# Sigmoid attention and a mixture-of-depths block on one core: values loaded earlier into borrowed tiles, an earlier ranking, shared sums, and the last spot transfer on SyncE

## The chip, the cores and the metric

The kernel runs on one core of a Trainium2 chip. The metric is the device time of the program in microseconds, as the median of several runs; smaller is better. The kernel before takes 488.92 us (three runs, 486.96 to 489.0). Its profiled execution took 486.84 us, of which 485.0 us lie between the first and the last instruction. All times on the profile's clock count from that first instruction.

## The reference

Two stages follow each other, all in float32. The first is attention with a sigmoid in place of the softmax, over 8 batches (called blocks here), 12 heads, 448 tokens and 64 numbers per head:

```python
scores = scale * np.matmul(q, k.transpose(0, 1, 3, 2)) - np.log(S)
attn = 1.0 / (1.0 + np.exp(-scores))
attn_out = np.matmul(attn, v)
x = attn_out.transpose(0, 2, 1, 3).reshape(B, S, H * D)   # 8 x 448 x 768
```

The second picks, in each block, the 128 tokens with the largest score `x @ w_gate`, sends only those through a two-layer network (768 to 1024 to 768, with a ReLU between), weights the result with the sigmoid of the score and adds it to those rows. All other rows of `x` go to the output as they are:

```python
scores = np.einsum('bsd,d->bs', x, w_gate)
top_idx = np.argpartition(-scores[b], capacity)[:capacity]
xe = x[b, top_idx]
ye = np.maximum(xe @ w1, 0.0) @ w2
out[b, top_idx] = xe + sigmoid(scores[b, top_idx])[:, None] * ye
```

## The kernel before

**Steps and units.** The 12 heads of a block are three groups of four heads. Two groups make a step `s`, so there are 12 steps (0 to 11), and a block ends after one and a half steps. A step has seven units `n` (0 to 6). `unit(s, n)` multiplies keys with queries for a part of the key rows of both groups (line 280) and lets ScalarE put the sigmoid into tiles `attn_d` and `attn_u` (line 288). `values(s, n)` multiplies these with v in four quarters (line 315): quarter 0 runs in the last unit of its own step, quarters 1 to 3 in the units 0 to 2 of the next step. After quarter 3 VectorE takes the result out of the two banks `o` by transposes (`take`, line 330), and `gate_part` sums it against `w_gate` (lines 338 and 341).

**Loads.** Keys and queries of group `i` come through `load(i)` (line 100) and are turned on VectorE by `turn(i)` into `kT` and `qT` (lines 255 to 262). Values of step `s` come through `load_v(s)`: four transfers into `raw_v` (line 119) and four into `raw_h` (line 121). Both tiles exist once, so v of a step can be loaded only when quarter 3 of the step before has read the old one. For that reason `load_v(s)` stands in unit 3 of step `s`, and v is wanted in unit 6 of the same step. All of these are issued by SyncE in the order of the program. Each issue also waits until the transfer which had its completion counter before, eight transfers earlier in most cases, has landed.

**Routing.** When the last group of block `b` is done, `gate(b)` forms the 448 scores and GpSimd writes them to DRAM (line 366); `spread` reads them back as `rep`, once for every partition (line 378). `ranking` compares (`rank`, lines 386 and 389), and `place` turns the ranks, writes them to DRAM as `ranks` (line 399) and reads them back for every partition as `spot` (line 401). `choose` finds from `spot` which row goes to which of the 128 places (line 413), and GpSimd gathers these rows of `x_d`, a copy of `x` in DRAM, into a tile `xe` (line 426). There are three `xe` tiles; the last block uses an attention tile instead. In `routed` the steps of this chain are put into fixed units of later steps.

**The network.** Two blocks form a pair `p`. `turn_rows` transposes the gathered rows on TensorE (line 448). Both layers are multiplied with seven products of half-size blocks in place of eight: `first` (line 487) and `second` (line 552), with sums on VectorE. Six of the quarters of `w1` and `w2` lie in SBUF (`w1_sb`, `w2_sb`). The other eight operands are sums of quarters. `make_sum` forms each once on VectorE (line 172) in a region of the tile `hidden` or `rows_t`, and GpSimd writes it to DRAM (line 174). The table `SUMS` says in which unit. Later `lend` loads a sum into attention tiles that are free in that step (line 188), and `weight` hands it to a product and forgets it. The tables `WORK` and `LENT` say which products and loads lie in which unit. Pairs 0 and 1 and the start of pair 2 run beside the attention.

**The end.** `rest` is written out by hand: the rest of pair 2, the routing of block 7, the products of pair 3, and the copies of blocks 6 and 7 to the output (line 351), followed by the scatter of the computed rows (line 572). An engine does its instructions in the order in which the program gives them.

Of the kernel before, what the change touches and what calls it, by code (L numbers as in the profile page):

```python
# [9 lines left out]
F32 = mybir.dt.float32  # L10
# [7 lines left out]
def kernel(  # L18
# [85 lines left out]
    def load_v(s):  # L104


        if s >= NS:
            return
        raw_v[s] = (vals.tile([P, 8, NF * Dh], F32, name="raw_v"),
                    vals.tile([P, 4, Dh], F32, name="raw_h"))  # L110
        tv, th = raw_v[s]

        def blocks(h, r, nh, n):
            return bass.AP(tensor=v.tensor,
                           offset=v.offset + (8 * s + h) * S * Dh + r * Dh,
                           ap=[[TB * Dh, TT], [S * Dh, nh], [1, n * Dh]])

        for m in range(4):
            nc.sync.dma_start(out=tv[m * TT:(m + 1) * TT], in_=blocks(0, NF * m, 8, NF))
        for n in range(4):  # L120
            nc.sync.dma_start(out=th[n * TT:(n + 1) * TT],
                              in_=blocks(4 * (n // 2), HK + n % 2, 4, 1))
# [3 lines left out]


    QW = KH * FH * P
    assert QW == FH * DH and QW % (2 * P) == 0 and FH * DH // 2 % DH == 0
    w1_sb = const.tile([P, 3, QW], F32, name="w1_sb")  # L130
    w2_sb = const.tile([P, 3, QW], F32, name="w2_sb")
# [20 lines left out]

    room = {}

    def load_left(m):

        if m == 1:
            t = moe.tile([P, 7 * FH * P], F32, name="hidden")
            room["a"], room["b"] = t[:, :QW], t[:, QW:2 * QW]
        load_quarter(m, room["a"], (1, 0) if m == 1 else (0, 1))  # L160

    def make_sum(m, key):
        if (m, key) == (1, 6):
# [11 lines left out]


    SUMS = {(1, 3): (1, 5), (1, 4): (1, 6), (1, 5): (1, 7), (1, 6): (1, 3),
            (2, 4): (2, 5), (2, 5): (2, 6), (2, 6): (2, 7), (3, 0): (2, 4)}

    def attn_tile(pr, slot):  # L180
        return attnp.tile([P, 2, S], F32, name=f"attn{pr}_{slot}")
# [7 lines left out]
            halves.append(t)  # L189
        lent[m, key] = halves  # L190

    def weight(m, key):

        if (m, key) in lent:
            halves = lent.pop((m, key))
            return lambda o, n: halves[2 * o // QW][:, o % (QW // 2):o % (QW // 2) + n]
        x = {(1, 1): 0, (1, 2): 1, (1, 4): 2, (2, 1): 0, (2, 2): 1, (2, 3): 2}[m, key]
        return lambda o, n: (w1_sb, w2_sb)[m - 1][:, x, o:o + n]
# [92 lines left out]
    def values(s, n):  # L291

        tv, th = raw_v[s]
        if n == 0:
            outs[s] = [banks(0), banks(1)]
        o = outs[s]
        first = (0, 2, 2, 0)[n]  # L300
        quads = [(first + m) % 4 for m in range(4)]
        work = [(r, c) for c in range(NF) for r in quads]
        if n < 2:
            at = 4 * (NF - 1)
            work[at:at] = [(r, None) for r in quads]
        for r, c in work:
            x, pr = divmod(r ^ n, 2)
            rows = slice(r * TT, (r + 1) * TT)
            for j in range(2):
                if c is None:  # L310
                    w, a = th[rows, 2 * pr + j, :], attn[s, pr, NF]
                else:
                    w = tv[rows, 4 * x + 2 * pr + j, c * Dh:(c + 1) * Dh]
                    a = attn[s, pr, (NF + 1) * x + c]
                nc.tensor.matmul(o[x][j * Dh:(j + 1) * Dh, pr, :S], w, a[rows, j, :],  # L315
                                 start=(n == 0 and c == 0), stop=(n == 3 and c == NF - 1))
        if n < 3:
            nc.scalar.activation(o[x][Dh:Dh + 1, pr, S:S + 1], bias_s[Dh:Dh + 1], AF.Copy)
        else:
            for x in range(2):  # L320
                for pr in range(2):
                    take(s, pr, x)
# [67 lines left out]
            out=junk[:n], in0=rep[:n], scalar=own, in1=earlier[:n, c, :],  # L390
            op0=ALU.is_equal, op1=ALU.mult, accum_out=level[:n, c:c + 1])

    def place(b):

        nc.vector.tensor_add(place_s[:, :NC], above, level)
        by_col = moe.tile([P, TT], F32, name="by_col")
        nc.vector.transpose(by_col, place_s)
        ranks = dram.tile([P, TT], F32, name="ranks")
        nc.gpsimd.dma_start(out=ranks, in_=by_col)
        spot = moe.tile([P, 4, NC * TT], F32, name="spot")  # L400
        nc.gpsimd.dma_start(
            out=spot, in_=bass.AP(tensor=ranks.tensor, offset=ranks.offset,
                                  ap=[[0, P], [TT * TT, 4], [1, NC * TT]]))
        st[b]["spot"] = spot.rearrange("p m c -> p (m c)")[:, :S]
# [72 lines left out]
    def first(p, key, where="o"):  # L477
        n = CAP
        x = pairs[p]["x"][:, ROWS1[key]]
        if key == 1:  # L480
            t = moe.tile([P, 7 * FH * P], F32, name="hidden")
            pairs[p]["h"] = t.rearrange("p (m k n) -> p m k n", m=7, k=FH)
        w = weight(1, key)
        ps = bank(where).rearrange("p (k n) -> p k n", n=P)
        for f in range(FH):
            for t in range(KH):
                nc.tensor.matmul(ps[:, f, :n], w((t * FH + f) * P, P), x[:, t, :n],  # L487
                                 start=(t == 0), stop=(t == KH - 1))
        if key == 2:
            pairs[p]["second"] = True  # L490
            last_row(p)
        return p, key, ps
# [53 lines left out]
    def second(p, key, where="o"):  # L546
        n = CAP
        h = pairs[p]["h"][:, ROWS2[key]]
        w = weight(2, key)
        ps = bank(where)  # L550
        for t in range(FH):
            nc.tensor.matmul(ps[:n, :DH], h[:, t, :n], w(t * DH, DH),  # L552
                             start=(t == 0), stop=(t == FH - 1))
        return p, key, ps
# [59 lines left out]
    def put(s, n, fn, *args):  # L614
        late.setdefault((s, n), []).append((fn, args))

    def routed(b):

        s = (NG * b + NG - 1) // 2 + 1
        if s == NS:  # L620
            return
        put(s, 4, spread, b)
        put(s, 4, store, b)
        put(s + 1, 1, ranking, b)
        if s + 2 <= NS:
            put(*((s + 2, 1) if b % 2 else (s + 1, 5)), copy_out, b)
            put(s + 2, 0, choose, b)

    def ranking(b):
        for c in range(NC):  # L630
            rank(b, c)
        place(b)

    def gates(i):
        gate_part(i)
# [26 lines left out]
    def rest():  # L662


        for n in range(3):
            gap(NS, n)
        p, b = NP - 2, B - 1
        for key, slot in (((1, 3), "d10"), ((2, 4), "d11")):
            lend(*key, slot)
        work = [(item, begin(item, "any")) for item in ((1, p, 6), (1, p, 7))]  # L670
        gates(2 * NS - 1)

        store(b, (0, 1))
        gate(waiting.pop())
        spread(b, nc.sync)
        store(b, (2, 3))
        for key, slot in (((2, 5), "d12"), ((2, 6), "u3"), ((2, 7), "u4")):
            lend(*key, slot)
        for item, args in work:
            finish(item, args)  # L680
        for key in (4, 5):
            do((1, p, key), "any")
        first_sums(*begin((1, p, 3), "any"), sums_too=())
        work = [((2, p, key), begin((2, p, key), "any")) for key in (2, 1, 4)]
        ranking(b)
        hidden_sum(p, 5)
        work.append(((2, p, 5), begin((2, p, 5), "any")))
        choose(b - 1)
        hidden_sum(p, 6)
        finish(*work[0])  # L690
        work.append(((2, p, 6), begin((2, p, 6), "any")))
        hidden_sum(p, 7)
        finish(*work[1])
        work.append(((2, p, 7), begin((2, p, 7), "any")))
        hidden_sum(p, 3)
        for item, args in work[2:]:
            finish(item, args)
        choose(b)
        do(("t", b - 1), "any")
        do((2, p, 3), "any")  # L700

        for key, slot in (((1, 3), "d12"), ((1, 6), "u3"), ((1, 7), "u4"), ((1, 5), "d00"),
                          ((2, 6), "d01"), ((2, 5), "d02"), ((2, 7), "d10"), ((2, 4), "d11")):
            lend(*key, slot)
        copy_out(b - 1)
        copy_out(b)
        p += 1
        for item in ((1, p, 1), (1, p, 2), ("t", b)):
            do(item, "any")
        work = [((1, p, key), begin((1, p, key), "any")) for key in (3, 6, 7)]  # L710
        for item, args in work[1:]:
            finish(item, args)
        first_sums(*work[0][1], sums_too=())
        for key in (4, 5):
            do((1, p, key), "any")
        for m in (5, 6, 7, 3):
            hidden_sum(p, m)
        for key in (1, 2, 6, 5, 3, 7, 4):
            do((2, p, key), "any")

    def stream():
# [14 lines left out]
        for s in range(NS):  # L736
            for n in range(NU):
                unit(s, n)
                if n == (0 if s == 0 else 1):
                    turn(2 * s + 1)  # L740
                    load(2 * s + 3)
                if n == 3 and s > 0:
                    load_v(s)
                gap(s, n)
                if n == NU - 2:
# [41 lines left out]
```

## Time and profile before

| | us | share of the span |
|---|---|---|
| median of the runs | 488.92 | |
| span of the profiled execution | 485.0 | |
| TensorE, matmul | 450.1 | 93% |
| TensorE, weight load (beside the matmuls) | 273.1 | 56% |
| VectorE | 298.9 | 62% |
| ScalarE | 181.6 | 37% |
| GpSimd | 50.1 | 10% |
| keys by queries, L280, 2496 matmuls | 154.5 | |
| attention by v, L315, 1152 + 1152 + 384 matmuls | 132.3 + 132.9 + 29.4 | |

Busy time is read as follows. Engines run beside each other, so the columns do not add to the span. Several of the small matmuls of L280 and L315 run in different parts of the array at once, and overlapping ones are counted once. The transfers of SyncE took 64.9% of the time of the 16 DMA engines over the span, those of GpSimd 12.5%. Together they moved 104.19 MB, most of it in small packets: 97344 of the 131085 packets are below 512 bytes.

Two kinds of view are used for the rest. A list of waits says which engine stood idle until which other had done something. A timeline gives instructions in the order of their start, with the idle time ahead of an instruction and what ended it in square brackets. "SPq" is the queue of SyncE: the time shown there is the issue of a transfer, with its waits for completion counters, and not the transfer itself. Where a wait is for several events, the one named is the one that came last by the profile.

### The profile page before, as it was taken

The numbers are of one execution on the slowest core, as the hardware profiler recorded it, in microseconds if no ns is written. First come the engines' busy times: TensorE is split into PE (matmuls) and PEld (weight loads), VectorE is DVE, ScalarE is ACT, GpSimd is POOL, SyncE is SP. The second block draws the span as 40 slices with busy tenths as digits, with TensorE's granted clock in tenths as the row PEclk, the third lists the DMA queues.
The fourth block names the chain that finished last, engine by engine and source line by source line (L and its number), as shares of the span: only waits on it lengthen the run. The fifth ranks groups of instructions, "written<-read, shape, count | busy, mean of one in ns | idle before, by whom it ended". The sixth has DMA issues, their size and how long they took to land. (4 is left out here: it accounts for less than half of the span.)

```text
span 485.0 us, 14374 instructions
## 1 busy us (share of the span) xinstructions
PE 450.1 (93%) x6326; PEld 273.1 (56%) x6326; DVE 298.9 (62%) x663; ACT 181.6 (37%) x237; POOL 50.1 (10%) x81
## 2 busy tenths in 40 slices
PE   8998979879999999999999999999999999748993
PEld 3553525426554664555477844685566386338951
DVE  4319495976552875985637576786618579812371
ACT  4746462443554345334355253344346201001100
POOL 8000001011000001011100000010100010210001
PEclk9999998999999999999999999999999999958999
DMA  8956998899948974999697848899459887998201
GB/s 262 325 219 168 372 284 252 229 203 238 250 128 301 211 179 102 269 184 336 154 333 199 141 158 225 160 256 318 130 175 244 134 197 155 277 354 305 97 0 65
DMA packets 131085, 104.19 MB, mean 215 GB/s; under 512 B 97344, under 2 KB 112000, under 8 KB 130768
## 3 DMA queue, kind: packets, MB, share of 16 engines
q1 hardware_dynamic: 126864, 86.75, 64.9%
q0 software_dynamic: 4160, 16.53, 12.5%
q8 instruction: 49, 0.80, 0.7%
q14 instruction: 12, 0.10, 0.1%
HBM read 82.67 MB, written 31.60 MB: 236 GB/s over the span
## 5 line engine op out<-in xcount | busy, mean ns | idle before, releaser
L280 PE MATMUL psc<-qT,kT 32*64 32x448 f32 x2496 | 154.5, 541 | 5.4 <-ACT attn_u L288 4.9
L315 PE MATMUL o<-attn_d,raw_v 32*64 32x448 f32 x1152 | 132.3, 543 | 2.9 <-DMA raw_v<-in_v_dram 2.3
L315 PE MATMUL o<-attn_u,raw_v 32*64 32x448 f32 x1152 | 132.9, 545 | 1.9 <-DMA raw_v<-in_v_dram 1.2
L288 ACT ACTIVATE attn_u<-psc,bias_s 128x896 f32<-128x896 f32 x86 | 81.9, 1004 | 83.1 <-PE psc L280 83.1
L280 PEld LDWEIGHTS psc<-qT,kT 32*64 32x64 f32 x2496 | 64.9, 131 | 64.7 <-issue 36.2
L288 ACT ACTIVATE attn_d<-psc,bias_s 128x896 f32<-128x896 f32 x70 | 66.7, 1003 | 49.2 <-PE psc L280 48.0
L330 DVE STREAM_TRANSPOSE x_b<-o 128x448 f32<-128x448 f32 x48 | 26.9, 617 | 79.5 <-PE o L315 79.5
L315 PEld LDWEIGHTS o<-attn_u,raw_v 32*64 32x64 f32 x1152 | 54.7, 133 | 30.0 <-issue 17.8
L315 PEld LDWEIGHTS o<-attn_d,raw_v 32*64 32x64 f32 x1152 | 50.5, 133 | 25.4 <-issue 15.3
L341 DVE TENSOR_REDUCE gate_p<-scr 128x14 f32<-128x448 f32 x48 | 29.8, 622 | 1.7
L552 PE MATMUL o<-attn_d,hidden 128*128 128x384 f32 x88 | 30.4, 492 | 0.0
L487 PEld LDWEIGHTS o<-rows_t,w_sb 128*128 128x128 f32 x240 | 27.6, 192 | 4.5 <-issue 1.4
L487 PEld LDWEIGHTS o<-rows_t,attn_d 128*128 128x128 f32 x240 | 27.5, 192 | 4.8 <-DVE rows_t L460 2.0
L338 DVE TENSOR_TENSOR scr<-x_b,wg_b 128x448 f32<-128x448 f32 x48 | 29.5, 614 | 1.0
L487 PE MATMUL o<-rows_t,attn_d 128*128 128x128 f32 x240 | 28.8, 277 | 1.2 <-DVE rows_t L460 1.2
L487 PE MATMUL o<-rows_t,w_sb 128*128 128x128 f32 x240 | 29.0, 278 | 0.4 <-DVE rows_t L454 0.3
L563 DVE SCALAR_TENSOR_TENSOR xe<-o,gate,xe 128x384 f32<-128x384 f32 x37 | 21.1, 612 | 13.4 <-PE o L552 13.3
L315 PE MATMUL o<-attn_u,raw_h 32*64 32x448 f32 x384 | 29.4, 555 | 0.0
L500 DVE TENSOR_TENSOR hidden<-o,hidden 128x512 f32<-128x512 f32 x23 | 15.3, 688 | 22.6 <-PE o L487 22.3
L255 DVE STREAM_TRANSPOSE kT<-raw_k 128x384 f32<-128x384 f32 x46 | 23.6, 552 | 7.4 <-DMA raw_k<-in_k_dram 3.8
L503 ACT ACTIVATE hidden<-hidden 128x512 f32<-128x512 f32 x12 | 7.5, 630 | 53.7 <-DVE hidden L500 53.7
L386 DVE TENSOR_SCALAR_CACHE_REDUCE scr<-rep,score 128x448 f32<-128x448 f32 (+1 forms) x32 | 21.5, 671 | 9.2 <-DMA rep<-scores 8.3
(102 smaller groups left out, 419.8 us busy)
## 6 DMA issues: line engine op xcount, KB each, us to landing
attn_d<-sum SPq DMA_DIRECT2D x56, 384.0 KB
x_d<-x_b SPq DMA_DIRECT2D x32, 336.0 KB
out_dram<-x_d SPq DMA_DIRECT2D x8, 1344.0 KB
raw_k<-in_k_dram SPq DMA_DIRECT2D x23, 448.0 KB
raw_q<-in_q_dram SPq DMA_DIRECT2D x23, 448.0 KB
raw_v<-in_v_dram SPq DMA_DIRECT2D x48, 192.0 KB
w_sb<-in_moe_w_dram SPq DMA_DIRECT2D x6, 768.0 KB
sum<-hidden POOLq DMA_DIRECT2D x6, 768.0 KB, 7.1
```

Of the source, the lines that this page charges most:

```text
L255: nc.vector.transpose(kT[i][:, e, :HK], sk[:, e, :HK].rearrange("p (m c) d -> p c m d", c=NF))
L280: nc.tensor.matmul(psc[h // 2][y * Dh:(y + 1) * Dh, h % 2, :S], kT[2 * s + x][d, e, r:r + 2, :].rearrange("d r t -> d (r t)"), qT[2 * s + ...
L288: nc.scalar.activation(a, psc[pr][:, :, :S], AF.Sigmoid, bias=bias_s, scale=QK_SCALE)
L315: nc.tensor.matmul(o[x][j * Dh:(j + 1) * Dh, pr, :S], w, a[rows, j, :], start=(n == 0 and c == 0), stop=(n == 3 and c == NF - 1))
L330: nc.vector.transpose(x_tiles[b][:, :, 2 * g + pr, :], outs[s][x][:, pr, :S].rearrange("p (r t) -> p r t", t=TT))
L338: nc.vector.tensor_tensor(out=tmp, in0=x_tiles[b][:, :, hp, :], in1=wg_b[:, hp:hp + 1, :].to_broadcast([P, TB, TT]), op=ALU.mult)
L341: nc.vector.tensor_reduce(out=gate_parts[b][:, :, hp], in_=tmp, axis=AX.X, op=ALU.add)
L386: nc.vector.tensor_scalar(out=junk[:n], in0=rep[:n], scalar1=own, scalar2=0.0, op0=ALU.is_gt, op1=ALU.add, accum_out=above[:n, c:c + 1])
L487: nc.tensor.matmul(ps[:, f, :n], w((t * FH + f) * P, P), x[:, t, :n], start=(t == 0), stop=(t == KH - 1))
L500: nc.vector.tensor_tensor(out=dst, in0=a, in1=b, op=ALU.add)
L552: nc.tensor.matmul(ps[:n, :DH], h[:, t, :n], w(t * DH, DH), start=(t == 0), stop=(t == FH - 1))
L563: nc.vector.scalar_tensor_tensor(out=xe[:n, cols], in0=ps[:n, :DH], scalar=st[b]["gate"][:n, 0:1], in1=xe[:n, cols], op0=ALU.mult, op1=ALU ...
```

## The change

There are four parts.

1. Values of steps 1 and 3 no longer go into `raw_v` and `raw_h` but into two of the three `xe` tiles (half of the heads each) and a free part of the first `hidden` tile, behind the two regions that the sums use. Those places are not needed by the routed blocks until later. So v alternates between two places in the first five steps, and `load_v` of steps 1 to 4 is issued one step earlier: that of step 1 at the end of step 0, those of steps 2, 3 and 4 in unit 3 of the step before. From step 5 on all is as it was. The main part of v comes in eight transfers in place of four in steps 1 and 3, with the same bytes.
2. The ranking of block 0 moves from unit 1 of step 3 to the last unit of step 2. Two of the sums, (2, 7) and (2, 4), move from unit 6 of step 2 and unit 0 of step 3 to units 4 and 5 of step 3.
3. The sums loaded for pair 2 stay in their tiles, and pair 3 uses them there. The eight `lend` calls for pair 3 in `rest`, which make 16 transfers of 384 KB, are gone.
4. In the routing of the last block SyncE issues the `spot` transfer, and no longer GpSimd.

Line numbers in the profile of the changed kernel are up to 18 higher than those above.

```diff
@@ load_v
-        raw_v[s] = (vals.tile([P, 8, NF * Dh], F32, name="raw_v"),
-                    vals.tile([P, 4, Dh], F32, name="raw_h"))
-        tv, th = raw_v[s]
+        if s in (1, 3):
+            tv = [moe.tile([P, D], F32, name="xe", bufs=3).rearrange("p (h c) -> p h c", h=4)
+                  for _ in range(2)]
+            at = 2 * QW + s // 2 * 4 * Dh
+            th = room["all"][:, at:at + 4 * Dh].rearrange("p (h c) -> p h c", h=4)
+        else:
+            t = vals.tile([P, 8, NF * Dh], F32, name="raw_v")
+            tv = [t[:, :4], t[:, 4:]]
+            th = vals.tile([P, 4, Dh], F32, name="raw_h")
+        raw_v[s] = (tv, th)
...
-            nc.sync.dma_start(out=tv[m * TT:(m + 1) * TT], in_=blocks(0, NF * m, 8, NF))
+            rows = slice(m * TT, (m + 1) * TT)
+            if s in (1, 3):
+                for x in range(2):
+                    nc.sync.dma_start(out=tv[x][rows], in_=blocks(4 * x, NF * m, 4, NF))
+            else:
+                nc.sync.dma_start(out=t[rows], in_=blocks(0, NF * m, 8, NF))
@@ SUMS
-            (2, 4): (2, 5), (2, 5): (2, 6), (2, 6): (2, 7), (3, 0): (2, 4)}
+            (2, 4): (2, 5), (2, 5): (2, 6), (3, 4): (2, 7), (3, 5): (2, 4)}
@@ weight
-    def weight(m, key):
+    def weight(m, key, p):
         if (m, key) in lent:
-            halves = lent.pop((m, key))
+            halves = lent[m, key]
+            if p != NP - 2:
+                del lent[m, key]
@@ place
-    def place(b):
+    def place(b, queue=nc.gpsimd):
...
-        nc.gpsimd.dma_start(
+        queue.dma_start(
             out=spot, in_=bass.AP(tensor=ranks.tensor, offset=ranks.offset,
@@ routed
-        put(s + 1, 1, ranking, b)
+        put(*((s, NU - 1) if b == 0 else (s + 1, 1)), ranking, b)
@@ rest
-        ranking(b)
+        ranking(b, nc.sync)
...
-        for key, slot in (((1, 3), "d12"), ((1, 6), "u3"), ((1, 7), "u4"), ((1, 5), "d00"),
-                          ((2, 6), "d01"), ((2, 5), "d02"), ((2, 7), "d10"), ((2, 4), "d11")):
-            lend(*key, slot)
         copy_out(b - 1)
         copy_out(b)
@@ stream
-                if n == 3 and s > 0:
+                if (n == NU - 1 and s == 0) or (n == 3 and s in (1, 2, 3)):
+                    load_v(s + 1)
+                elif n == 3 and s > 4:
                     load_v(s)
```

More of the change, by code (lines that the diff above doesn't have):

```diff
@@ L128 @@
     QW = KH * FH * P
+    assert D == 4 * NF * Dh and 2 * QW + 8 * Dh <= 7 * FH * P
     assert QW == FH * DH and QW % (2 * P) == 0 and FH * DH // 2 % DH == 0
@@ L153 @@
     room = {}
+    room = {}
     def load_left(m):
@@ L158, in load_left @@
             t = moe.tile([P, 7 * FH * P], F32, name="hidden")
-            room["a"], room["b"] = t[:, :QW], t[:, QW:2 * QW]
+            room["all"], room["a"], room["b"] = t, t[:, :QW], t[:, QW:2 * QW]
         load_quarter(m, room["a"], (1, 0) if m == 1 else (0, 1))
@@ L312, in values @@
                 else:
-                    w = tv[rows, 4 * x + 2 * pr + j, c * Dh:(c + 1) * Dh]
+                    w = tv[x][rows, 2 * pr + j, c * Dh:(c + 1) * Dh]
                     a = attn[s, pr, (NF + 1) * x + c]
@@ L482, in first @@
             pairs[p]["h"] = t.rearrange("p (m k n) -> p m k n", m=7, k=FH)
-        w = weight(1, key)
+        w = weight(1, key, p)
         ps = bank(where).rearrange("p (k n) -> p k n", n=P)
@@ L548, in second @@
         h = pairs[p]["h"][:, ROWS2[key]]
-        w = weight(2, key)
+        w = weight(2, key, p)
         ps = bank(where)
@@ L627, in routed, with ranking @@
             put(s + 2, 0, choose, b)
-    def ranking(b):
+    def ranking(b, *queue):
         for c in range(NC):
             rank(b, c)
-        place(b)
+        place(b, *queue)
     def gates(i):
```

## The prediction

> **What bounds the kernel now.** I began with the page. TensorE is busy for 93% of the span, so only its idle and slowed time can be won.
>
> ```profile
> PE 450.1 (93%) x6326; PEld 273.1 (56%) x6326; DVE 298.9 (62%) x663; ACT 181.6 (37%) x237; POOL 50.1 (10%) x81
> PEclk9999998999999999999999999999999999958999
> ```
>
> The next view is the list of waits of TensorE alone. The columns are total us, times, longest.
>
> ```profile
> PE o L448 <- DMA xe<-x_d,row: 8.3, 1, 8.3
> ...
> PE o L315 <- DMA raw_v<-in_v_dram: 3.5, 5, 1.3
> PE o L280 <- DVE x_b L330: 2.1, 1, 2.1
> ```
>
> One wait of 8.3 us stands out; the others are small, but a list of waits does not show slowed matmuls. So I took busy time in stretches: one each for steps 1, 2 and 3 of the attention (counted from 0), then two in the last part. After the stretch and its length come busy us of TensorE, weight load, VectorE, ScalarE and GpSimd, then TensorE's granted clock, DMA share and GB/s.
>
> ```profile
> 21.40:47.20 25.80, 24.38 (x466) 12.55 (x450) 11.87 (x18) 13.72 (x17) 1.20 (x2) 1.00 0.63 205
> 47.20:77.60 30.40, 26.98 (x460) 12.11 (x454) 22.64 (x38) 13.72 (x17) 3.23 (x6) 0.94 0.97 296
> 77.60:111.10 33.50, 28.02 (x460) 14.09 (x451) 25.03 (x62) 13.72 (x17) 4.51 (x7) 0.95 0.95 238
> ...
> 422.50:431.00 8.50, 0.25 (x2) 0.29 (x3) 2.65 (x8) 0.00 (x0) 1.00 (x1) 0.63 1.00 267
> 431.00:441.40 10.40, 10.40 (x62) 8.62 (x61) 0.62 (x1) 1.50 (x3) 1.97 (x2) 0.81 1.00 394
> ```
>
> Steps 1 to 3 hold the same TensorE work (460 to 466 matmuls), yet last 25.8, 30.4 and 33.5 us. Steps 2 and 3 lose 4.6 and 7.7 us against step 1: part is idle, part a TensorE clock of 0.94 and 0.95. DMA is 0.95 to 0.97 full there and 0.63 in step 1. The timeline says what ended the idle time:
>
> ```profile
> 60.55 4.02 SPq L119 DMA_DIRECT2D raw_v<-in_v_dram  x4
> 64.61 6.12 SPq L121 DMA_DIRECT2D raw_h<-in_v_dram  x4
> ...
> 71.49 1.62 PE L315 MATMUL o<-attn_d,raw_v 32*64 32x448 f32 x8 [1.27 <-DMA raw_v<-in_v_dram]
> ...
> 94.12 2.34 PE L280 MATMUL o<-qT,kT 32*64 32x448 f32 x26 [2.08 <-DVE x_b L330]
> ...
> 103.47 1.73 PE L315 MATMUL o<-attn_d,raw_v 32*64 32x448 f32 x8 [1.07 <-DMA raw_v<-in_v_dram]
> ```
>
> Step 2's v was issued from 60.55 to 70.7 for matmuls ready at 70.2. In step 1 that quarter of values takes 3.4 us (43.75 to 47.15). In step 2 it takes 7.4 (70.2 to 77.6), in step 3 8.7 (102.4 to 111.1): late v costs 4.0 and 5.3 us, slow matmuls included.
>
> Last, the timeline of the final part:
>
> ```profile
> 412.38 0.57 POOL L399 DMA_DIRECT2D ranks<-by_col  x1 [11.78 <-DVE by_col L397]
> ...
> 420.35 0.75 POOL L401 DMA_DIRECT2D spot<-ranks  x1 [7.41 <-DVE xe L563]
> 421.41 1.02 POOL L426 DMA_INDIRECT xe<-x_d,row  x1 [0.30 <-DMA attn_d<-sum]
> ...
> 428.82 0.69 DVE L413 SCALAR_TENSOR_TENSOR scr<-spot,slot,number 128x448 f32<-128x448 f32 x1 [5.15 <-DMA spot<-ranks]
> ...
> 430.75 1.51 PE L448 MATMUL o<-iden,xe 128*128 128x128 f32 x6 [8.26 <-DMA xe<-x_d,row]
> ```
>
> The gather of block 6's rows (L426) had its row numbers at 414.0, but stood on GpSimd behind the `spot` transfer of block 7, which waited for `ranks` to land. So it was issued at 421.4, landed 9.3 us later, and TensorE stood still from 422.5 to 430.75.
>
> **What the Trainium skill says.** "TensorE: Matmul & The Clock Gate", section "What's actually happening": about 3.4 us of idle time halve the clock until the array has been busy as long again. The trace agrees: after the 8.26 us gap eight matmuls of L552 take 4.20 us, elsewhere 2.74. "DMA: Bandwidth & Descriptors", section "Issuing engines are not separate DMA queues": transfers of all issuers share the same 16 DMA engines, so another issuer saves issue time alone. The trace can only half agree: here it is not issue time but the order behind a wait that costs. "Perfetto Trace Analysis", section "Tensor Engine Instruction (MATMUL, LD_WEIGHTS)": GpSimd and VectorE work strictly in order. The 7.4 us of L426 behind L401 are that.
>
> **The change part by part.** Times are on the clock of before.
>
> *`spot` of the last block on SyncE.* The gather can be issued right behind `ranks`, at about 414.1. The indirect gathers landed in 3.0 to 9.2 us, median 5.8; six loads of sums are still draining, so I take 8: 422.1, before TensorE wants it at 422.5 (ends: 417 and 423.3). SyncE has nothing else to do then but the two copies to the output, which wait for a scatter at 427 or later, so the new wait delays nobody. `ranks` lands at 420.3 as before, or some us sooner. No 256 KB `spot` on SyncE is in the trace; bounds are the 3.3 us from SyncE's `rep` of 224 KB (402.56) to its reader (405.88), and GpSimd's 6.8 to 8.6 us. I take 4: 424.3. Two selections and two conversions 1.5 us, gather at 425.8, landed after 5.8: 431.6. TensorE's road there: turning block 6 from 422.5, 0.9; one second-layer product 2.74; two first-layer products of 2.84 each: 431.8. It was 441.44: gain 9.6 us, that is 8.26 of wait and 1.4 of slow clock. At the slow bound `spot` costs 4 of them.
>
> *Shared sums.* 16 loads of 384 KB vanish from 414 on. TensorE shows no wait for them after 441, so alone they give nothing; they clear the road for `ranks`, `spot` and both gathers. Counted as 0.
>
> *v earlier.* Issued one step earlier for steps 1 to 4, v lies ready. v(1) goes behind the weights from 19 us and is needed at 43.75: free. v(2) goes out at about 35, where DMA is 0.63 full. v(3) takes the place of v(2) in the busy stretch, with eight main transfers for four, but nobody waits for it until about 100. Step 2: values end at 73.6 for 77.6. The next scores need qT of group 6, which VectorE finishes only at 74.5, as before: gain 3.1, not 4.0.
>
> *First ranking earlier.* On VectorE it now stands ahead of turn 7. Its `rep` was issued at 75.19 and needs 4.9 to 5.7 us: 80.5. VectorE then does 6.4 us of ranks (86.9), turn 7 in 2.2 (89.1), and the four transposes in 2.2 (91.3). TensorE wants turn 7 at 74.5 + 12.65 = 87.1: it waits 2.0, then 0.7 for its bank, against the 2.1 it waited for `x_b` before. So 0.6 is lost. The two sums (1.75 us each), moved behind it, sit where VectorE's next product, turn 8, is ready at 103.0, when TensorE arrives.
>
> *Step 3.* With v there, the 5.3 us go too. Step 4 starts at 103.0 for 111.1: 8.1 gained, or 3.1 - 0.6 + 5.3 = 7.8; I keep 8.
>
> *Step 4 gives some back.* Block 1's scores leave at 98.4 for 102.1, only 3.7 sooner (the transposes ahead of them start at 89.1 for 92.83); its `rep` landed 12.3 us later (114.4): 110.7. Ranks end at 116.9, the transposes that free the bank for turning block 0 at 119.1, where TensorE arrives at 117.2. I take 1.5; ends 0 and 5, the latter if the two moved sums (1.5 MB at 238 GB/s, 6 us) push `rep` back. From there on TensorE has no wait worth naming until 411, so what is gained stays.
>
> Sum: 9.6 + 8.0 - 1.5 = 16.1; 488.9 - 16.1 = 472.8 us.
>
> **The rivals.**
> A: only the end gains. The chain scores, `rep`, ranks, turn runs on DMA latency and VectorE's order, and eats the 6.5 us of the body. For it: DMA is 0.95 full in that stretch, VectorE has 25 of 33.5 us in step 3. Against: it was late by only 2.1 before. 488.9 - 9.6 = 479.3.
> B: only the body gains: `spot` or the gather lands late, so that one of the turns still waits. For it: 9.3 us of landing in the trace. Against: the loads which filled DMA then are gone. 488.9 - 6.5 = 482.4.
> C: nothing is given back, all losses of steps 2 and 3 (4.6 + 7.7) and 9.6 go: 467.0.
> D: slower: `ranks` holds `spot` on SyncE as long as before (0 at the end), and the ranking ahead of turn 7 plus the sums beside block 1's `rep` cost 4 + 6 more than the 8.0: 491.
>
> **How the numbers follow.** Forecast 0.62, A 0.14, B 0.08, C 0.12, D 0.04. The bounds above put the forecast between 468 (no giving back, early `rep`) and 478 (`spot` 4 later, or step 4 at 5). With C at the low end and A at the high end the range is 467 to 480. Faster by over 0.5%: all but D and a sliver of B, 0.94; same 0.02; slower 0.04.
>
> **What would show it.** Right: no wait on L448 over 1.5 us; the values of steps 2 and 3 without a DMA wait, those steps near 27 and 29 us; a wait of 2 to 3 us for qT or kT of turn 7 and about 1.5 for `x_b` in step 4; the last four output products starting as far after the second turn as now. Wrong: the gather of block 6 landing after 8 us or more past its new issue, or TensorE waiting for turn 7 or block 1's ranking for over 5 us.

## The result and the profile after

The changed kernel takes 472.06 us at the median (471.45 to 480.11, four runs) for 488.96 before: the ratio is 0.966 with a 95% interval of 0.962 to 0.969. The forecast was 472.8. The span of the profiled execution went from 485.0 to 469.7 us. On the chips of the experiments single executions of one kernel scatter by several us (before: 481.2 to 499.4), so below medians are over all executions of a kernel, ratios over its least disturbed ones (within 1.5% of its fastest; the traces of e1 and e8 are of executions beyond that), and I read each mechanism from a stretch of the trace.

TensorE's waits after the change, in total us, times, and longest (lines up to 18 higher than before: L298 is keys by queries, L466 the turns of gathered rows, L570 the second layer):

```profile
PE psc L298 <- DVE qT L280: 6.1, 3, 3.2
...
PE psc L570 <- DVE hidden L552: 1.8, 1, 1.8
...
PE o L466 <- DMA attn_u<-x_d,row: 0.2, 1, 0.2
```

The wait of 8.3 us for the gathered rows is gone; all that is left on that line is 0.2 us for the second gather. So are the waits for v and for `x_b` in step 3. In their place stands a kind that hardly existed: 6.1 us for turned queries. The stretches of steps 1 to 4 (columns as before):

```profile
21.40:47.30 25.90, 24.48 (x446) 13.92 (x438) 12.42 (x19) 13.68 (x18) 1.20 (x2) 0.93 0.83 245
47.30:75.70 28.40, 25.61 (x492) 14.43 (x478) 19.67 (x37) 14.17 (x19) 2.53 (x5) 1.00 0.93 298
75.70:102.30 26.60, 23.71 (x452) 11.72 (x454) 23.04 (x53) 13.74 (x17) 2.57 (x5) 1.00 0.91 213
102.30:135.20 32.90, 29.44 (x503) 17.64 (x504) 21.21 (x47) 15.86 (x21) 4.04 (x6) 1.00 0.94 234
```

Steps 2 and 3 went from 30.4 and 33.5 us to 28.4 and 26.6, at a full clock. Step 4 went from 30.1 (111.1 to 141.2 before) to 32.9, with TensorE busy for 29.4 of it. That is where a part is given back. The timeline there:

```profile
104.42 14.95 SPq L366 DMA_DIRECT2D x_d<-x_b  x4
119.42 5.63 SPq L369 DMA_DIRECT2D out_dram<-x_d  x1
125.15 0.53 SPq L100 DMA_DIRECT2D raw_k<-in_k_dram  x1
...
132.64 1.04 DVE L273 STREAM_TRANSPOSE kT<-raw_k 128x384 f32<-128x384 f32 x2 [4.58 <-DMA raw_k<-in_k_dram]
...
135.19 2.61 PE L298 MATMUL psc<-qT,kT 32*64 32x448 f32 x32 [3.23 <-DVE qT L280]
...
141.42 1.74 PE L298 MATMUL psc<-qT,kT 32*64 32x448 f32 x32
```

and before, on SyncE:

```profile
103.49 11.03 SPq L348 DMA_DIRECT2D x_d<-x_b  x4
114.57 3.06 SPq L351 DMA_DIRECT2D out_dram<-x_d  x1
117.73 0.53 SPq L100 DMA_DIRECT2D raw_k<-in_k_dram  x1
```

The keys of group 10 were issued at 125.2, behind 20.6 us of stores and copies on SyncE. VectorE waits 4.6 us for them, TensorE 3.2, and its next matmuls are slow: the first 32 take 2.61 us where 1.76 is usual, and from their start to the 32 of the next unit (141.42) it is 6.2 us where 4.5 is usual. Together that is 4.9 us. TensorE is 8.8 us ahead of before at the start of step 4 and 4.7 at the start of step 6, so 4.1 us are given back net. Before, the same load went out at 117.7 and nobody waited. It now comes later in two ways: 7.4 us by the clock, and measured against TensorE, which is earlier, from 6.6 us into step 4 to 22.9.

The final part, after:

```profile
409.34 0.57 POOL L417 DMA_DIRECT2D ranks<-by_col  x1 [13.19 <-DVE by_col L415]
...
411.80 1.02 POOL L444 DMA_INDIRECT xe<-x_d,row  x1 [1.90 <-DVE hidden L556]
...
414.96 2.85 PE L570 MATMUL psc<-attn_u,hidden 128*128 128x384 f32 x8
...
415.28 0.37 SPq L419 DMA_DIRECT2D spot<-ranks  x1
...
417.64 0.82 PE L466 MATMUL o<-iden,xe 128*128 128x128 f32 x6
...
420.02 0.68 DVE L431 SCALAR_TENSOR_TENSOR scr<-spot,slot,number 128x448 f32<-128x448 f32 x1
...
426.58 0.84 PE L466 MATMUL o<-iden,attn_u 128*128 128x128 f32 x6 [0.18 <-DMA attn_u<-x_d,row]
```

and two lines of before:

```profile
419.67 2.82 PE L552 MATMUL psc<-attn_u,hidden 128*128 128x384 f32 x8
...
441.44 0.82 PE L448 MATMUL o<-iden,attn_u 128*128 128x128 f32 x6
```

The gather of block 6 (L444) is issued 2.5 us after `ranks`, not 9.0. The wait for `ranks` is now on SyncE (415.28), where only the output copies stand behind it. The first turn needs no wait, and the second stands 11.6 us after the last product of pair 2 ahead of the first turn (414.96 to 426.58), where it was 21.8 (419.67 to 441.44).

### The profile page after: what moved, and what is told of

It is laid out like the page before. It is cut to its first block, busy times and chain, and to the rows that moved or that the text cites. A ratio compares the mean times of both kernels' runs of the same rounds, so it can differ in the third digit from the quotient of the medians.

```text
span 469.7 us, 14366 instructions
## 1 busy us (share of the span) xinstructions
PE 443.4 (94%) x6326; PEld 276.8 (59%) x6326; DVE 299.0 (64%) x663; ACT 181.8 (39%) x237; POOL 49.7 (11%) x80
## 5 line engine op out<-in xcount | busy, mean ns | idle before, releaser
L298 PE MATMUL psc<-qT,kT 32*64 32x448 f32 x2496 | 155.5, 546 | 10.9 <-DVE qT L280 6.1
L333 PE MATMUL o<-attn_d,raw_v 32*64 32x448 f32 x960 | 108.5, 540 | 0.4 <-ACT o L336 0.4
L298 PEld LDWEIGHTS psc<-qT,kT 32*64 32x64 f32 x2496 | 66.7, 132 | 69.8 <-issue 42.7
L333 PE MATMUL o<-attn_u,raw_v 32*64 32x448 f32 x960 | 106.3, 540 | 0.8 <-ACT o L336 0.8
L333 PEld LDWEIGHTS o<-attn_u,raw_v 32*64 32x64 f32 x960 | 46.9, 133 | 20.2 <-issue 13.5
L333 PEld LDWEIGHTS o<-attn_d,raw_v 32*64 32x64 f32 x960 | 45.6, 133 | 16.8 <-issue 13.0
L505 PEld LDWEIGHTS o<-rows_t,attn_d 128*128 128x128 f32 x264 | 30.3, 192 | 4.7 <-DVE rows_t L478 1.9
L505 PE MATMUL o<-rows_t,attn_d 128*128 128x128 f32 x264 | 31.6, 277 | 1.1 <-DVE rows_t L478 1.1
L518 DVE TENSOR_TENSOR hidden<-o,hidden 128x512 f32<-128x512 f32 x23 | 15.3, 688 | 22.2 <-PE o L505 21.9
L570 PE MATMUL o<-attn_d,hidden 128*128 128x384 f32 x80 | 27.6, 493 | 0.0
L333 PE MATMUL o<-attn_d,xe 32*64 32x448 f32 x192 | 26.1, 563 | 0.0
```

The lines of the kernel that those rows point to most:

```text
L298: nc.tensor.matmul(psc[h // 2][y * Dh:(y + 1) * Dh, h % 2, :S], kT[2 * s + x][d, e, r:r + 2, :].rearrange("d r t -> d (r t)"), qT[2 * s + ...
L518: nc.vector.tensor_tensor(out=dst, in0=a, in1=b, op=ALU.add)
L570: nc.tensor.matmul(ps[:n, :DH], h[:, t, :n], w(t * DH, DH), start=(t == 0), stop=(t == FH - 1))
```

## The experiments

Two stretches serve as measures, both read from TensorE's timeline. *Body*: from unit 6 of step 1 (at 42.01 before) to the third first-layer product of pair 0 (161.06 before). *End*: from the product (2, 2, 5) (412.76 before) to the second turn (441.44 before). Each is of one trace for each run. The pieces are e1 to e4 and e6, e11; e7 to e10 and e12 are variants of the changed kernel.

| run | median us (before, same chip) | ratio, 95% interval | body | end |
|---|---|---|---|---|
| before | | | 119.1 | 28.7 |
| changed | 472.1 (489.0) | 0.966, 0.962 to 0.969 | 114.2 | 16.9 |
| e1 spot on SyncE alone | 483.5 (489.3) | 0.985, 0.980 to 0.990 | 122.0 | 21.0 |
| e2 shared sums alone | 486.8 (489.3) | 0.988, 0.982 to 0.994 | 116.1 | 23.5 |
| e3 both of the end | 479.8 (489.3) | 0.985, 0.967 to 1.002 | 123.5 | 17.2 |
| e4 v and ranking | 483.8 (489.3) | 0.995, 0.992 to 0.999 | 115.2 | 26.1 |
| e5 changed, again | 471.2 (488.8) | 0.973, 0.966 to 0.979 | 114.4 | 16.8 |
| e6 v alone | 485.4 (488.8) | 1.000, 0.996 to 1.003 | 117.3 | 26.6 |
| e7 keys first | 464.6 (488.8) | 0.956, 0.950 to 0.962 | 110.8 | 16.8 |
| e8 keys first, sums after | 467.2 (488.8) | 0.961, 0.955 to 0.967 | | |
| e9 keys first, again | 466.6 (489.5) | 0.958, 0.950 to 0.966 | 111.1 | 16.8 |
| e10 sums after | 472.9 (489.5) | 0.972, 0.963 to 0.981 | 116.4 | 16.8 |
| e11 ranking alone | 491.7 (489.5) | 1.011, 1.004 to 1.019 | 122.5 | 25.9 |
| e12 sums where they were | 470.7 (488.6) | 0.969, 0.961 to 0.977 | 113.6 | 16.7 |

The end is steady: 16.7 to 17.2 us wherever both of its changes are in, 25.9 to 28.7 where neither is. The 28.7 of the kernel before is the odd one of the latter four: TensorE waits there for a loaded sum and takes 6.9 us from product (2, 2, 5) to (2, 2, 7), 5.2 in every other trace; the other three have 25.9 to 26.6. The body of the kernel before is not steady: 116.1 to 123.5 in its four traces (before, e1 to e3).

**e1, e2, e3: the end in parts.** The edits, each on the kernel before (e3 has both):

```diff
-        ranking(b)
+        ranking(b, nc.sync)              # e1, e3
...
-        for key, slot in (((1, 3), "d12"), ((1, 6), "u3"), ...
-            lend(*key, slot)             # e2, e3; pair 3 uses pair 2's tiles
```

> Only the last spot transfer moves to SyncE; all 16 late loads of sums stay, behind it on SyncE. Theory (order on GpSimd): the gather of block 6 is issued near 414 and not 421, the wait of 8.3 us at the first turn of the end is gone; the loads start some 6 us later but TensorE needs them late enough. Gain 6 to 10 us: 479 to 483. Rival (DMA crowded by the loads): issued sooner, the gather still lands near 428 or later, gain below 3 us: 486 or more.

> Only the 16 late loads of sums are left out (pair 3 uses the tiles of pair 2); spot stays on GpSimd. Theory (order on GpSimd): the gather of block 6 is still issued only after ranks has landed, at 418 to 420, and lands in about 6 us and not 9: gain 3 to 5 us, 484 to 486. Rival (crowding): ranks, spot and gather all land early, the wait of 8.3 us shrinks below 2: 480 to 482.

> Both changes of the end and nothing of the attention part. Theory: the end gains as in the changed kernel, where the second turn stands 10.1 us sooner against the last product of pair 2: 478.9, give or take 1. Rival (the end gains only because the attention part shifted the transfers): less than 8 us, above 481.

The end of e1, `spot` on SyncE with all the loads kept:

```profile
418.68 1.02 POOL L426 DMA_INDIRECT xe<-x_d,row  x1 [1.90 <-DVE hidden L538]
...
437.64 1.52 PE L448 MATMUL o<-iden,attn_u 128*128 128x128 f32 x6 [4.36 <-DMA attn_u<-x_d,row]
```

and that of e2, the loads left out with `spot` on GpSimd:

```profile
416.62 0.76 POOL L403 DMA_DIRECT2D spot<-ranks  x1 [5.36 <-DVE xe L565]
417.68 1.02 POOL L428 DMA_INDIRECT xe<-x_d,row  x1 [0.30 <-DVE xe L565]
...
423.30 1.51 PE L450 MATMUL o<-iden,xe 128*128 128x128 f32 x6 [4.14 <-DMA xe<-x_d,row]
```

In e1 the gather follows `ranks` (416.21) by 2.5 us and the first turn does not wait at all; but with the loads in the way the second gather, issued at 430.75, is 4.4 us late. In e2 the gather still comes 7.0 us behind `ranks` (410.69), but lands in 5.6 us for 9.3: the wait shrinks from 8.3 to 4.1. Against the three steady traces with the old end (mean 26.2), the end gains 5.1 us in e1, 2.7 in e2 and 9.0 with both; against the kernel before, with its odd wait, it would be 7.7, 5.2 and 11.5. The three ratios are alike (0.985, 0.988, 0.985), so it is this stretch, and not the run times, that shows the two parts adding up.

Both causes are seen in the traces. GpSimd's order held the gather: it is issued 2.5 us behind `ranks` in e1, 7.0 in e2. And with the late loads the transfers of this part land slowly: the first gather took 8.4 to 9.2 us in the four traces with the old end and 3.9 to 5.5 in those without the loads, the second 6.9 to 7.3 against 3.9 to 4.1. In e1 the first gather is issued ahead of the loads and took 4.1. `ranks` itself gained nothing, with 5.2 to 7.4 us against 5.2 to 6.3. `spot` took 7.2 to 8.4 us on GpSimd with the loads and 5.6 in e2; on SyncE 6.2 in e1 and 4.7 to 4.8 without them. Neither theory alone was right; mine was nearer, as it allowed for 3 to 5 in e2, though both medians lie a little above what I had expected (483.5 for 479 to 483, 486.8 for 484 to 486).

The shared sums may be worth a little more behind the second turn. The first product there, 24 matmuls behind a wait, takes 4.4 to 5.5 us in some traces and 2.9 in the others. Before, e2 and changed:

```profile
444.09 4.50 PE L487 MATMUL psc<-rows_t,attn_d 128*128 128x128 f32 x24 [1.83 <-DVE rows_t L454]
...
437.21 2.94 PE L489 MATMUL psc<-rows_t,attn_d 128*128 128x128 f32 x24 [1.83 <-DVE rows_t L456]
...
428.89 4.57 PE L505 MATMUL psc<-rows_t,attn_d 128*128 128x128 f32 x24 [1.46 <-DVE rows_t L472]
```

It is slow in all five traces with the late loads and in two of the nine without (changed and e8). No run here shows why. But the wait right ahead of it is 1.2 to 1.8 us long whether it is slow or not, and at step 5 slow matmuls followed a wait of 3.2 us. So in this kernel matmuls are slow behind waits shorter than the 3.4 us that the prediction quotes; here the measurement decides.

**e4, e6, e11: the body in parts.** e4 is the earlier v with the earlier ranking and the two moved sums, on the old end; e6 the earlier v alone; e11 the ranking and the sums alone.

```diff
-        put(s + 1, 1, ranking, b)
+        put(*((s, NU - 1) if b == 0 else (s + 1, 1)), ranking, b)      # e4, e11
...
+                if (n == NU - 1 and s == 0) or (n == 3 and s in (1, 2, 3)):
+                    load_v(s + 1)                                      # e4, e6
```

> Earlier v with the earlier ranking and the two moved sums, nothing of the end. Theory: steps 2 and 3 gain about 9 us as in the changed kernel, of which step 5 gives 4 back through late keys of group 10: gain 4.7, so 484.3; the end keeps its 8.3 us wait. Rival (all of it given back before the end): within 1 us of before, 488 to 490.

> Earlier v alone on the kernel before: the first ranking and the two sums are where they were, and nothing of the end is changed. Theory (the earlier ranking is what lets TensorE keep the gain): the ranking stands right ahead of the transposes that free the banks of unit 4 of step 3, TensorE comes 2 to 3 us sooner and so waits 4 to 5 us for x_b where it waited 2.1, and block 0's choice holds VectorE at the start of step 4; the body gains 1 to 3 us less than with the ranking moved: 485 to 487 with the old end. Rival (the ranking's place is worth nothing): the same as values and ranking together, 484.

(The name of e6 is misleading: its end is the old one, as the text says.)

> The kernel before with the earlier ranking and the two moved sums alone; v and the end are as before. Theory: the 2.1 us wait for x_b in step 3 goes, but TensorE comes only sooner to the late v of step 3: gain 0 to 1 us, 488 to 489. Rival (ranking alone is worth what it is worth with v): 2 to 3 us, 486.

e4 shows what was expected: no wait for v, 2.4 us for group 10, a body of 115.2. In e6 the body is 117.3: TensorE waits 2.5 us for `x_b` in step 3 and 1.2 for it at the first turn of block 0. I had expected 4 to 5 at the first of these. By these two traces the place of the ranking and the sums is worth 2 us of the body with v; the runs (483.8 and 485.4, on two chips, with ratios that overlap) are too near to each other to show it. Without v it is worth nothing; TensorE's timeline in e11:

```profile
104.07 1.76 PE L315 MATMUL o<-attn_d,raw_v 32*64 32x448 f32 x6 [4.26 <-DMA raw_v<-in_v_dram]
```

The wait for `x_b` is gone and the wait for v has grown to 4.3 us. The time was no better, 1.011 with an interval above 1, so a little worse than my 488 to 489.

The ratios of e4 and e6 are close to 1 though their medians are 5.5 and 3.4 us below that of before. By the ratio the body's part is worth about 2 us (e4) or nothing (e6). What earlier v mainly narrows is the spread: e4 took 480.8 to 491.0 us and e6 481.1 to 488.9, before on the same chips 482.1 to 499.4 and 481.2 to 495.3. A likely reason: the kernel before has executions in which v comes nearly in time. The trace of e2 is one; its body code is that of before, and TensorE does not wait for v in step 3 at all (the 1.2 us are in step 2):

```profile
PE o L282 <- DVE x_b L332: 3.6, 1, 3.6
...
PE o L317 <- DMA raw_v<-in_v_dram: 1.2, 1, 1.2
```

In e3, with the same body code, the same list has

```profile
PE o L317 <- DMA raw_v<-in_v_dram: 9.0, 2, 6.4
```

So the body is better judged on the new end, where e3 is the kernel without the body's parts: 479.8 us (four runs, 475.6 to 484.2), against 472.1 and 471.2 for the changed kernel (e5: 469.3 to 474.1), with before alike on their chips (488.8 to 489.3).

**e5, e7, e9: keys ahead of the stores.** The changed kernel with two places altered, so that SyncE issues the load of group 10 before the copies of blocks 1 and 0:

```diff
-        put(s, 4, store, b)
+        put(s, NU - 1 if b == 1 else 4, store, b)
...
-            put(*((s + 2, 1) if b % 2 else (s + 1, 5)), copy_out, b)
+            put(*((s + 2, 1) if b % 2 or b == 0 else (s + 1, 5)), copy_out, b)
```

> The changed kernel as it is, on the same chip as the three others of this set, as their mark: 472 by both theories, and the same wait of about 3 us for the queries of group 10 at the start of step 5.

> The changed kernel, with the copy of block 1 to DRAM (unit 4 to unit 6 of step 3) and the copy of block 0 to the output (unit 5 of step 3 to unit 1 of step 4) put behind the load of group 10 on SyncE. Theory (the changed kernel gives back 4 us at step 5 because these keys stand behind 15 us of stores): the wait for group 10 is gone, 468 to 469. Rival (DMA itself is the limit there, in whatever order): the wait moves to the block 1 gather or to other keys, within 1 us of the changed kernel.

> Keys first once more, with more rounds, beside the next two. Theory: 3.5 to 4 us below the changed kernel, so 467 to 468, or a few us less as in its first measurement (464.6); against before 20 to 24 us. Rival: the first measurement was luck, within 1.5 us of the changed kernel, 470 to 472.

SyncE's queue in e7:

```profile
107.74 0.35 SPq L100 DMA_DIRECT2D raw_k<-in_k_dram  x1
108.27 1.35 SPq L100 DMA_DIRECT2D raw_q<-in_q_dram  x1
109.67 13.74 SPq L366 DMA_DIRECT2D x_d<-x_b  x4
```

The keys go out at 107.7 for 125.2, the start of step 5 has no wait, and the body is 110.8 and 111.1 for 114.2 and 114.4. So 3.4 of the 4.1 us that the changed kernel gives back were SyncE's order, and can be had. The medians are 6.6 us (e7, same set as e5) and 4.6 (e9, against e5) below the changed kernel, where I had expected 3 to 4; the first is more than the body shows, and the rest I can't place. On the chip of e5 and e7 the two ratios do not overlap (0.966 to 0.979 and 0.950 to 0.962), so this version beats both kernels.

**e8, e10, e12: where the sums stand.** In e8 and e10 the sums of `w2` follow the turns of groups 6 and 8 (e8 on keys first, e10 on the changed kernel). In e12 the two moved sums are back where they were.

```diff
-            (2, 4): (2, 5), (2, 5): (2, 6), (3, 4): (2, 7), (3, 5): (2, 4)}
+            (2, 5): [(2, 5), (2, 6)], (3, 5): [(2, 7), (2, 4)]}                 # e8, e10
+            (2, 4): (2, 5), (2, 5): (2, 6), (2, 6): (2, 7), (3, 0): (2, 4)}     # e12
```

> As keys first, and the four sums of w2 stand behind the turns of groups 6 and 8 on VectorE (two each in unit 5 of steps 2 and 3). Theory: the waits of 1.4 and 1.5 us for the queries of groups 6 and 8 go too: 1.5 to 3 us less than keys first, 465 to 467. Rival (TensorE then only waits for the next item of the chain, the first ranking or the turn of group 7): no more than 0.5 us less.

> The changed kernel with the four sums of w2 behind the turns of groups 6 and 8, and nothing else. Theory: the 1.4 and 1.5 us waits for these queries go, but TensorE then comes sooner to the keys of group 10, which are late by SyncE's order alone, and waits there for longer by as much: within 1 us of the changed kernel, 471 to 472. Rival (each wait counts by itself): 2 to 3 us less, 469.

> The changed kernel with the sums (2, 7) and (2, 4) back in unit 6 of step 2 and unit 0 of step 3, behind the early ranking on VectorE. Theory (the moved sums lengthen the stores of block 1, and so hold the keys of group 10): these four stores take about 11 us on SyncE and not 14 to 15, the wait for group 10 falls from 3 us to below 1.5; but the two sums now hold turn 7, and TensorE waits 2 to 3 us in unit 3 of step 3. Time within 2 us of the changed kernel. Rival (the stores are long because TensorE runs ahead, wherever the sums are): they still take 14 us or more, the wait of 3 us stays and the time grows by 2 to 3 us.

e8 is not better than keys first (467.2 for 464.6 and 466.6); the intervals overlap, and its trace is of an execution of 473.0 us, far above its median, so I leave it open. e10 shows how waits move: the wait for group 6 is gone, but group 7 now costs 1.5, group 8 3.1 and group 10 2.2, and the list says

```profile
PE psc L298 <- DVE qT L280: 7.3, 4, 3.1
```

for 6.1 before the edit; the time stays. In e12:

```profile
91.02 1.36 PE L298 MATMUL psc<-qT,kT 32*64 32x448 f32 x20 [1.75 <-DVE qT L280]
...
108.16 10.25 SPq L366 DMA_DIRECT2D x_d<-x_b  x4
...
135.97 1.76 PE L298 MATMUL psc<-qT,kT 32*64 32x448 f32 x32 [0.62 <-DVE qT L280]
```

The stores of block 1 take 10.3 us on SyncE (11.0 before, 15.0 changed), the wait for group 10 falls to 0.6, and turn 7 now holds TensorE for 1.8. So the moved sums, 1.5 MB written just as block 1 is stored, are what lengthened the issue of those stores. Moving them bought turn 7 and paid with group 10; the time is the same, 470.7.

## Why the prediction was right, point by point

- **The end: right, mechanism and size.** Forecast 9.6 us between the last product of pair 2 ahead of the first turn and the second turn, measured 10.2 (21.8 to 11.6), or 9.1 to 9.7 against the other three traces with the old end (20.7 to 21.3). By terms: `ranks` at 420.3 "or some us sooner" landed 5.9 us after its issue, not 8; `spot` on SyncE, taken as 4, lies between 3.3 and 8.6 as bounded (in e3 from 424.26 to its reader at 429.01, 4.8 with a wait at the end); the gather, taken as 8, was there within 5.8 (411.80 to 417.64). The landing times that I quoted, "3.0 to 9.2 us, median 5.8", mix gathers with scatters. The seven gathers alone took 4.8 to 9.2, median 6.4; with that the sum for the second gather would have been 0.6 us longer, and it took at most 4.2 (422.36 to 426.58). "Alone they give nothing", of the shared sums, was too low: alone they took 4.1 us of the wait in e2. In the sum this did little harm, since I had counted the cleared road in part in the landing times. The sign that I had named for what follows, the last output products as far after the second turn as now, held within 0.4 us (43.6 to 43.2 us from the second turn to the end).
- **v: right in the mechanism, the two sizes off against each other.** No wait for v is left. Step 2 gains 2.0 us where I had 3.1: all of VectorE's work for group 6 came 1.1 us later than before, not "as before", and the wait for it, 0.9 in my sum, is 1.4. Step 3 gains 6.9 where I had 4.7 with the ranking's cost taken off.
- **"Free", of v(1), is open.** The way from the first matmul to unit 6 of step 1, ahead of *body*, takes 35.8 to 36.1 us in the five traces without the early v(1). With it, four have the same (35.6 to 36.4, the changed kernel too), but five have 37.2 to 38.3. No run singles out the cause.
- **The earlier ranking: direction right, size wrong.** I had 2.7 us of waits left in step 3 (turn 7 and a bank). There is none: `rep` was read at 78.6, not 80.5, and VectorE even stood idle for 1.1 us ahead of the four transposes. About half of it comes back at the turn of group 8, which costs 1.5 us where I had 0. Step 4 starts 8.8 us sooner; I had 8.
- **"Step 4 gives some back": the term that was mis-sized, and for the wrong reason.** I had 1.5 us from block 1's ranking, with an upper end of 5 if the moved sums pushed `rep` back. The ranking cost at most 0.2. The 4.1 us net came later, at the start of step 5, from keys that I had not followed: load 10 on SyncE behind the stores. The moved sums were the right suspect and the stores their victim (e12). "From there on TensorE has no wait worth naming until 411" failed by this, and by 1.4 more at 409.7, where VectorE's ranking of block 7 came later in relation to TensorE.
- **The sum.** 16.1 forecast. In the profiles: body 4.9, end 11.8, less 1.7 between them (1.4 of it the wait at 409.7), and 0.3 elsewhere: 15.3; between medians 16.9. That the total came so near was partly luck: 1.7 of the end's 11.8 is the odd wait in the trace of before, and the errors of the body (6.5 forecast, 4.9 to 5.6 found, the latter from the mean of the traces with the old body, 120.2, and the new, 114.6) and of the end (9.6 forecast) offset each other.
- **The rivals.** A (only the end gains, 479.3) and B (only the body, 482.4) are in effect e3 and e4, which took 479.8 and 483.8; the changed kernel lies below both with 472.1 and 471.2, so neither half was lost. C (nothing given back, 467.0) failed for this change, but was nearer to what the code allows than I gave it: another kernel, keys first, comes to 464.6 and 466.6. D falls by the result.

## What to carry to other kernels

When a producer's late data is moved up, follow every queue that now comes due sooner, not only the chain that was edited: here the gain of 8.9 us in two steps met a load that stood in SyncE's order behind 20 us of stores. On an engine that works in order, a transfer that must wait for another belongs on a queue where nothing useful stands behind it, and loads that TensorE needs soon belong ahead of stores that nobody reads for long. A wait removed alone may only feed the next one (e10, e11), so changes that stand in one chain should be tried together as well as apart.

## What the runs showed that I had not expected

- The wait for v in the kernel before is no fixed cost. With the same body code, step 3 waited for it 0 us (e2) to 6.4 (e3) in single executions, with DMA 0.95 full there. So one trace does not price such a wait: the longest one for v was 1.3 us in the trace of before, 6.4 in e3, and in step 3 of e2 there was none.
- 1.5 MB of writes by GpSimd lengthened the issue of four stores of 336 KB on SyncE, waits for completion counters included, from 10.1 to 11.2 us (traces with the sums in their old place: before, e1, e2, e3, e6, e12) to 13.5 to 15.5 (with the sums moved beside them: changed, e4, e5, e10, e11).
